# An attention and MoE kernel on one core: the 96 stores of P to scratch issued by GpSimd instead of SP, with a new table of plan shifts

## The chip, the core and the metric

The kernel runs on one core of a Trainium2 chip. Its time is the device time of one execution in microseconds. TensorE (PE) multiplies, with its weight loads shown apart (PEld); VectorE (DVE) and ScalarE (ACT) do elementwise work; SyncE (SP) issues the DMAs; GpSimd (POOL) does little. All data are float32; products are made from float32r pieces.

## The reference

Eight batches, eight heads, 512 tokens and 32 states of 64 numbers. The attention reads states by tokens and tokens by states; the results are put together and go through a bilinear feed-forward layer:

```python
def _attn_ref(x, state):                       # x: 8x8x512x64, state: 8x8x32x64
    scores = scale * np.matmul(x, state.transpose(0, 1, 3, 2))
    a = softmax(scores)
    xread = np.matmul(a, state)
    scores2 = scale * np.matmul(state, x.transpose(0, 1, 3, 2))
    a2 = softmax(scores2)
    sread = np.matmul(a2, x)
    return np.concatenate([xread, sread], axis=2)

def _moe_ref(x, w_a, w_b, w_out):              # 4352 tokens x 512, d_ff = 1536
    a = x @ w_a
    b = x @ w_b
    return a * b @ w_out
```

Here `softmax` stands for the four lines that subtract the maximum, take the exponential and divide by the sum.

## The kernel before, in words

**P.** The tokens' part of the feed-forward layer is not computed from `xread`. Since `xread = a @ state`, the kernel multiplies the states by the weights first: P = state x (w_a, w_b), for every batch and head, and then `x @ w_a` of a batch is `a @ P`. The 1536 columns of the hidden layer are cut into six chunks (c = 0 to 5) of 256 columns of w_a and w_b each. For a chunk, `chunk(c)` converts the weights (`Conv`: shifts and merges on DVE, casts on ACT, a float32 split into two float32r pieces, `wq`), then `products(c, bg)` makes P for four batches at a time (bg = 0, 1, a "half-chunk"): 8 products of 128x512 on PE into PSUM, copied by ACT into a staging buffer (`sw_st`, `wo10` or `wo11`, four in turn), and stored to DRAM, `scr{c}_{bg}`, in two DMAs of 256 KB for each buffer: 8 stores for a half-chunk, 96 in all. The store is where the layout changes: rows leave in the order of states and batches and come back batch by batch.

**Loads of P.** `Batch.load(c)` reads the 512 KB of one batch and chunk from `scr` into `p_raw`; `split` makes the pieces `p_h` (cast on ACT) and `p_l` (difference on DVE). There are 46 such loads; two of the 48 (batch, chunk) pairs are made directly (`direct0`, `direct1`).

**The two layers.** `layer1` multiplies the attention weights `at_h`, `at_l` of a batch by P's pieces into PSUM `ab`, and ACT and DVE form the product of the two halves and split it (`a_sb`, `g_h`, `g_l`). `layer2` multiplies that by the pieces of w_out (`wo0` to `wo11`) into `acc`. The table `VISITS` says which batch takes which chunks when. Partial sums of a batch go to DRAM (`part`) and come back (`stg`). A last unit does the same for the states' own rows.

**The order.** Nothing is issued as the code is written. Every call is recorded as a unit with its engine; `Recorder.cost` gives it an occupancy and a latency; `plan` works out a latest time for each unit backwards from PE's paced matmuls, adds the unit's entry of the table `SHIFTS` (in 100 ns, by the unit's number), and then puts each engine's units in an order by these times. The engines run these orders; each instruction waits by semaphores for what it reads, and each engine's queue is in order. SP's queue issues all 279 rows of DMAs, loads and stores mixed; a store that waits for its copy holds up the loads behind it. GpSimd makes an identity matrix at the start and then nothing. Nearly every instruction is issued from one line of the source, so the profile shows one line number, and the tiles' names tell the work apart.

Of the kernel before, what the change touches and what calls it, by code (L numbers as in the profile page):

```python
# [167 lines left out]
class Recorder:  # L168
# [31 lines left out]
    def cost(self, u, eng, method, out, ins, kw):  # L200
        n = 1
        sh = (out if isinstance(out, View) else ins[0]).where()[0]
        for x in sh[1:]:
            n *= x
        ps = bool(ins) and ins[0].tile.pool.name.startswith("ps")
        if eng == "PE":
            if method == "transpose" or kw.get("is_transpose"):
                o = n * .85
            elif ins[-1].dtype == F32R:
                o = (n + 32) / 2.4  # L210
            else:
                o = n / .6
            if sh[0] < P:
                o *= sh[0] / P
            if method == "matmul" and "is_transpose" not in kw and ins[-1].dtype == F32 and not u.turned:
                o, u.turned = o + 370, True
            lat = o + 172
        elif eng == "ACT":
            if method == "activation":
                o, lat = (870, 960) if "accum_out" in kw else (560, 660)  # L220
            elif ps:
                o, lat = 466 * n / 512 + (60 if n < 300 else 0), 587 * n / 512 + (80 if n < 300 else 0)
            else:
                o, lat = 522 * n / 512, 100 + n * 1.015
            if n < 8:
                o, lat = 60, 80
        elif eng == "DVE":
            if method.startswith("tensor_scalar") and not ps:
                o, lat = (65, 140) if n <= 1 else (75, 166) if n <= 16 else (333 * n / 512, 419 * n / 512)
            elif method == "tensor_reduce":  # L230
                o, lat = 593, 676
            elif method == "transpose":
                o, lat = 628, 704
            elif method == "reciprocal":
                o, lat = (72, 154) if n == 1 else (162, 244)
            else:
                o, lat = 65 + n * 1.045, 155 + n * 1.045
        elif eng == "SP":
            o = 440
            v = out if isinstance(out, View) else ins[0]  # L240
            u.bytes = 4
            for x in v.where()[0]:
                u.bytes *= x
            u.load = isinstance(out, View) and out.tile.pool.name != "dram"
            u.serve, u.land = u.bytes / 428 + (0 if u.load or u.bytes < 4e5 else 240), 1560 if u.load else 900
            lat = 980 + u.serve + u.land
        else:
            o, lat = 1000, 1060
        if eng in ("ACT", "DVE") and out.tile.name.startswith("sd_") and len(out.where()[0]) == 4:
            o, lat = 2 * o, 2 * lat  # L250
        if eng in ("ACT", "DVE"):
            o, lat = o * SLACK, lat * SLACK
        if u.calls[:-1]:
            u.lat = u.occ + lat
            u.occ += o
        else:
            u.occ, u.lat = o, lat
# [8 lines left out]
class Engine:  # L266
# [13 lines left out]


SHIFTS = {
# [12 lines left out]
}  # L295


# [164 lines left out]
def attn_moe(ctx, tc, xt, xn, sd, wl, w_out, out):  # L462
# [97 lines left out]
    nxt = []  # L560
# [40 lines left out]
    def columns(c, hp, hh):  # L601

        if c:
            return [(slice(0, 512), w[c, hp][:, hh])]
        x = hp % 2 * 256
        return [(slice(f * 256, f * 256 + 256), w[0, f, hp // 2][:, hh, x:x + 256]) for f in range(2)]
# [4 lines left out]
    def project(c, hp, bg, hh, psp, tag):  # L611
        if hh == 0:
            name, bufs = SW[st["n"] % len(SW)]
            st[bg], st["n"] = proj.tile([P, 2, 512], F32, name=name, bufs=bufs), st["n"] + 1
        sw = st[bg]
        ps = psp.tile([P, 512], F32, name=tag)
        with rec.together(sw):
            for cols, r in columns(c, hp, hh):
                for k, s in enumerate((sd_h, sd_l)):
                    nc.tensor.matmul(ps[:, cols], lhsT=s[hp // 2][:, 2 * (hp % 2) + hh, bg], rhs=r,  # L620
                                     start=(k == 0), stop=(k == 1))
        nc.scalar.copy(out=sw[:, hh], in_=ps)
        if hh:
            h = 2 * (hp % 2)
            nxt.extend(lambda i=i: nc.sync.dma_start(
                out=scr[c][bg][hp // 2, :, h + i].rearrange("b n x -> n b x"), in_=sw[:, i]) for i in range(2))


# [412 lines left out]
    def products(c, bg, where=ms):  # L1041
        for hp in range(4):
            for hh in range(2):
                project(c, hp, bg, hh, *where)
        flush()
# [126 lines left out]
```

## Time and profile before

| | us |
|---|---|
| median of three runs | 700.57 |
| the runs | 702.35, 700.57, 700.18 |
| the profiled execution | 700.03 |
| its span | 698.2 |
| PE busy | 677.7 (97%) |
| DVE busy | 486.5 (70%) |
| ACT busy | 394.3 (56%) |
| POOL busy | 0.7 |

The busy times are unions of the engines' instructions in one profiled execution; PE's ends are modelled, so that a busy PE is not necessarily at its peak. The span goes from the program's first instruction to its last. The granted TensorE clock was full (0.999). DMAs moved 134 MB, 55% of the 16 engines' time, all of the kernel's own from SP's queue. The lines of the page and of the timelines are shown with the steps that use them.

### The profile page before, as it was taken

The numbers are of one execution on the slowest core, as the hardware profiler recorded it, in microseconds if no ns is written. First come the engines' busy times: TensorE is split into PE (matmuls) and PEld (weight loads), VectorE is DVE, ScalarE is ACT, GpSimd is POOL, SyncE is SP. The second block draws the span as 40 slices with busy tenths as digits, with TensorE's granted clock in tenths as the row PEclk, the third lists the DMA queues.
The fourth block names the chain that finished last, engine by engine and source line by source line (L and its number), as shares of the span: only waits on it lengthen the run. The fifth ranks groups of instructions, "written<-read, shape, count | busy, mean of one in ns | idle before, by whom it ended". The sixth has DMA issues, their size and how long they took to land.

```text
span 698.2 us, 10183 instructions
## 1 busy us (share of the span) xinstructions
PE 677.7 (97%) x3712; PEld 543.2 (78%) x3712; DVE 486.5 (70%) x947; ACT 394.3 (56%) x727; POOL 0.7 (0%) x6
## 2 busy tenths in 40 slices
PE   4899999999999999999999999999999999999997
PEld 1576767887878888788888877877798888988886
DVE  5999788889986775745997367558869734884321
ACT  6988967898764667754543344334555433552322
POOL 0000000000000000000000000000000000000000
PEclk9999999999999999999999999999999999999999
DMA  8689977899495757768995144234244312500002
GB/s 325 243 295 336 338 248 243 307 319 393 163 335 204 271 171 251 252 232 263 392 332 158 59 155 125 95 120 139 82 152 150 109 43 61 181 31 30 1 0 92
DMA packets 55090, 134.36 MB, mean 192 GB/s; under 512 B 5632, under 2 KB 5632, under 8 KB 55040
## 3 DMA queue, kind: packets, MB, share of 16 engines
q1 hardware_dynamic: 55040, 133.71, 55.1%
q8 instruction: 29, 0.48, 0.3%
q14 instruction: 21, 0.17, 0.1%
HBM read 87.03 MB, written 46.66 MB: 191 GB/s over the span
## 4 chain that ended last, share of the span: by engine, by line
PE 88%; ACT 5%; DMA 5%; issue 1%; SPq 1%; DVE 0%; DVEq 0%
PE ab L1129 41%; PE acc L1129 38%; PE ms L1129 9%; ACT wq L1129 2%; DMA p_raw<-scr 1%; DMA p_raw<-sd 1%; DMA scr<-sw_st 1%; DMA part<-stg 1%; DMA scr<-wo 1%; SPq L1129 1%; ACT t L1129 1%; ACT sd_h L1129 0%; ACT wo L1129 0%; ACT sw_st L1129 0%; ACT g_h L1129 0%
## 5 line engine op out<-in xcount | busy, mean ns | idle before, releaser
L1129 PE MATMUL acc<-wo,g_h 128*128 128x512 f32 x816 | 249.0, 392 | 0.0
L1129 PEld LDWEIGHTS acc<-wo,g_h 128*128 128x128 f32 x816 | 151.6, 188 | 31.7 <-issue 0.8
L1129 DVE TENSOR_TENSOR a_sb<-ab,a_sb 128x512 f32<-128x512 f32 (+1 forms) x108 | 71.2, 659 | 130.2 <-PE ab L1129 115.2
L1129 PE MATMUL ab<-at_h,p_h 128*128 128x512 f32 x384 | 149.7, 394 | 2.4 <-ACT p_h L1129 2.4
L1129 PE MATMUL acc<-wo,g_l 128*128 128x512 f32 x408 | 150.9, 392 | 0.0
L1129 PE MATMUL ab<-at_l,p_h 128*128 128x512 f32 x384 | 149.6, 393 | 0.0
L1129 PE MATMUL ab<-at_h,p_l 128*128 128x512 f32 x384 | 148.8, 392 | 0.0
L1129 ACT COPY a_sb<-ab 128x512 f32<-128x512 f32 (+1 forms) x108 | 61.0, 565 | 137.6 <-PE ab L1129 137.0
L1129 ACT CAST g_h<-a_sb 128x512 fp32r<-128x512 f32 (+1 forms) x108 | 64.7, 599 | 59.5 <-DVE a_sb L1129 50.1
L1129 PEld LDWEIGHTS acc<-wo,g_l 128*128 128x128 f32 x408 | 76.6, 188 | 19.1 <-issue 2.5
L1129 DVE TENSOR_TENSOR g_l<-a_sb,g_h 128x512 fp32r<-128x512 f32 (+1 forms) x108 | 70.7, 655 | 28.1 <-ACT g_h L1129 21.3
L1129 PEld LDWEIGHTS ab<-at_h,p_h 128*128 128x128 f32 x384 | 72.2, 189 | 23.2 <-ACT p_h L1129 3.5
L1129 PEld LDWEIGHTS ab<-at_h,p_l 128*128 128x128 f32 x384 | 72.3, 189 | 16.0 <-issue 0.8
L1129 PEld LDWEIGHTS ab<-at_l,p_h 128*128 128x128 f32 x384 | 72.2, 189 | 15.3 <-issue 0.8
L1129 ACT CAST p_h<-p_raw 128x512 fp32r<-128x512 f32 x92 | 53.4, 621 | 24.5 <-PE ab L1129 16.0
L1129 DVE TENSOR_TENSOR p_l<-p_raw,p_h 128x512 fp32r<-128x512 f32 x92 | 60.1, 682 | 6.0 <-ACT p_h L1129 5.8
L1129 DVE TENSOR_SCALAR t<-t 128x512 int32<-128x512 int32 x120 | 49.6, 420 | 13.4 <-ACT t L1129 10.8
L1129 ACT CAST wq<-t 64x512 fp32r<-64x512 f32 (+1 forms) x64 | 38.7, 619 | 4.4 <-PE ab L1129 1.7
L1129 DVE SCALAR_TENSOR_TENSOR t<-raw,t 128x512 int32<-128x512 int32 (+1 forms) x60 | 39.5, 684 | 0.2
L1129 PE MATMUL ms<-wq,sd_h 128*128 128x512 f32 (+2 forms) x112 | 38.0, 412 | 0.3 <-ACT a L1129 0.2
L1129 PE MATMUL ms<-wq,sd_l 128*128 128x512 f32 (+2 forms) x112 | 37.4, 403 | 0.0
L1129 DVE TENSOR_TENSOR stg<-acc,stg 128x512 f32<-128x512 f32 x44 | 28.4, 683 | 9.2 <-PE acc L1129 9.2
(97 smaller groups left out, 671.4 us busy)
## 6 DMA issues: line engine op xcount, KB each, us to landing
p_raw<-scr SPq DMA_DIRECT2D x46, 512.0 KB, 4.0
scr<-sw_st SPq DMA_DIRECT2D x48, 256.0 KB, 5.1
scr<-wo SPq DMA_DIRECT2D x48, 256.0 KB, 4.2
raw<-wl SPq DMA_DIRECT2D x22, 512.0 KB, 6.1
part<-stg SPq DMA_DIRECT2D x20, 512.0 KB, 5.6
stg<-part SPq DMA_DIRECT2D x20, 512.0 KB, 5.0
out<-stg SPq DMA_DIRECT2D x34, 256.0 KB, 2.1
x_raw<-xt SPq DMA_DIRECT2D x14, 576.0 KB, 4.0
```

What stands on the lines that cost most here:

```text
L1129: getattr(obj, method)(*map(real, args), **{k: real(x) for k, x in kw.items()})
```

## The change

The stores of P are issued on GpSimd's queue; the recorder's cost function gets a branch for them; and the table of shifts is another one throughout, since the units are numbered anew when the stores are no longer SP's. The kernel's work is otherwise the same: the same matmuls, conversions, loads and stores.

```diff
@@ Recorder.cost
             else:
                 o, lat = 65 + n * 1.045, 155 + n * 1.045
+        elif method == "dma_start" and eng == "POOL":
+            o, lat = 1000, 3600
         elif eng == "SP":
             o = 440
...
@@ the table (16 lines before, 16 after; first line of each)
 SHIFTS = {
-    2: -1852, 7: 155, 8: 101, 12: 125, 13: -1927, 18: -166, 24: 194, 25: 125, 27: 16, 28: -291, 35: 29, 36: 59,
...
+    1: -726, 7: 339, 8: -507, 9: 151, 12: 165, 14: 29, 15: 900, 17: -215, 18: 169, 19: -256, 20: 2, 21: -113,
...
@@ project
         if hh:
             h = 2 * (hp % 2)
-            nxt.extend(lambda i=i: nc.sync.dma_start(
+            nxt.extend(lambda i=i: nc.gpsimd.dma_start(
                 out=scr[c][bg][hp // 2, :, h + i].rearrange("b n x -> n b x"), in_=sw[:, i]) for i in range(2))
```

The order moves on every engine. Three places, each as it stands in the built program (engine's rows in order; the number behind a name is the buffer's; x2 is two equal ones).

First, SP's queue around the first eight stores of P and the first loads of it, before:

```order
L1129 DMA raw_416<-wl 128x2x512
L1129 DMA scr0_0_466<-sw_st_447 32x4x512 x2
L1129 DMA scr0_0_466<-wo10_463 32x4x512 x2
L1129 DMA scr0_0_466<-sw_st_514 32x4x512 x2
L1129 DMA x_nat_557<-xn 128x1024
L1129 DMA scr0_0_466<-wo11_543 32x4x512 x2
L1129 DMA raw_594<-wl 128x2x512
L1129 DMA p_raw_627<-scr0_0_466 128x2x512
L1129 DMA p_raw_631<-scr0_0_466 128x2x512
```

SP's queue at the same place in the changed kernel:

```order
L1130 DMA raw_416<-wl 128x2x512
L1130 DMA wo6_433<-xn 128x1024
L1130 DMA raw_506<-wl 128x2x512
L1130 DMA x_nat_593<-xn 128x1024
L1130 DMA p_raw_622<-scr0_0_441 128x2x512
L1130 DMA p_raw_630<-scr0_0_441 128x2x512
```

and GpSimd's queue, which holds these stores first of all its DMAs:

```order
L1130 DMA scr0_0_441<-sw_st_427 32x4x512 x2
L1130 DMA scr0_0_441<-wo10_471 32x4x512 x2
L1130 DMA scr0_0_441<-sw_st_511 32x4x512
L1130 DMA scr0_0_441<-wo11_527 32x4x512
L1130 DMA scr0_0_441<-sw_st_511 32x4x512
L1130 DMA scr0_0_441<-wo11_527 32x4x512
```

The eight stores have left SP's queue; the same two loads, of weights and of x_nat, still stand ahead of the first loads of P.

Second, ACT's rows from the last copy of those eight products (`wo11<-acc`) to the first split of a loaded P, before:

```order
L1129 COPY wo11_543<-acc_547 128x512
L1129 ACTIVATE e2_499,m2_522<-e2_499,m2_522 128x512
L1129 COPY a_sb_580<-ab_361 128x512
L1129 ACTIVATE s_p_568<-s_p_568 128x512
L1129 ACTIVATE t1_600<-wo9_363 128x512
L1129 CAST at_h_609<-ms_584 128x512
L1129 CAST g_h_612<-a_sb_580 128x512
L1129 COPY a2_619<-ms_604 128x512
L1129 CAST at_l_623<-ms_584 128x512
L1129 ACTIVATE a2_619<-ms_633,m2_522 128x128
L1129 CAST p_h_680<-p_raw_627 128x512
```

and the last rows ahead of that split in the changed kernel:

```order
L1130 COPY stg_609<-acc_534 128x512
L1130 ACTIVATE s_p_598<-s_p_598 128x512
L1130 COPY stg_627<-acc_548 128x512
L1130 COPY sw_st_634<-ms_611 128x512
L1130 COPY stg_609<-acc_544 128x512
L1130 COPY stg_627<-acc_602 128x512
L1130 COPY sw_st_634<-ms_638 128x512
L1130 CAST at_h_659<-ms_646 128x512
L1130 CAST p_h_668<-p_raw_622 128x512
```

Four copies of sums to `stg` and two of the next half-chunk's products to `sw_st` stand ahead of the split, where before they stood behind it.

Third, DVE's rows at the last piece of chunk 0's weights (`wq_301`, now `wq_315`); `xst` is the states' result, `raw` is a load of w_out. Before:

```order
L1129 TENSOR_TENSOR sd_l1_241<-p_raw_108,sd_h1_179 128x4x4x32
L1129 TENSOR_SCALAR t1_229<-t1_229 128x512
L1129 TENSOR_SCALAR t2_325<-t1_313 128x512
L1129 SCALAR_TENSOR_TENSOR t1_229<-wo9_112,t1_229 128x512
L1129 SCALAR_TENSOR_TENSOR t2_325<-raw_196,t2_325 128x512
L1129 COPY xst_340<-ms_198 64x2x32 x2
L1129 TENSOR_SCALAR wo9_112<-t2_282 128x512
L1129 TENSOR_SCALAR t1_313<-t1_313 128x512
L1129 SCALAR_TENSOR_TENSOR wq_301<-t1_229,wo9_112 128x512
```

and in the changed kernel:

```order
L1130 TENSOR_TENSOR sd_l1_289<-p_raw_108,sd_h1_176 128x4x4x32
L1130 TENSOR_SCALAR wo9_119<-t2_284 128x512
L1130 TENSOR_SCALAR t2_343<-t1_301 128x512
L1130 SCALAR_TENSOR_TENSOR wq_315<-t1_262,wo9_119 128x512
L1130 TENSOR_SCALAR t1_301<-t1_301 128x512
L1130 TENSOR_TENSOR a_sb_341<-ab_269,a_sb_341 128x512
L1130 SCALAR_TENSOR_TENSOR t1_301<-raw_208,t1_301 128x512
L1130 SCALAR_TENSOR_TENSOR t2_343<-raw_208,t2_343 128x512
L1130 COPY xst_371<-ms_179 64x2x32
```

The two copies to `xst` and the merge and one shift of `w_out` (`t2<-raw`, `t1<-t1`) moved behind the weights' last piece.

21 rows, old and new, of the table SHIFTS are left out of this document.

## The prediction

> **What bounds the kernel now.** I read the page's first part, then the busy times in stretches that I chose by the loads of P, then the chain of waits, then the timelines of the engines that stand in it.
>
> ```profile
> span 698.2 us, 10183 instructions
> PE 677.7 (97%) x3712; PEld 543.2 (78%) x3712; DVE 486.5 (70%) x947; ACT 394.3 (56%) x727; POOL 0.7 (0%) x6
> ```
>
> PE is the bound over the whole, and GpSimd does nothing after the start. Windows (columns: length, then busy us and count of PE, weight loads, DVE, ACT, POOL, granted clock, DMA share, GB/s):
>
> ```profile
> 0.00:36.00 36.00, 22.69 (x168) 12.51 (x172) 27.07 (x59) 27.71 (x50) 0.70 (x6) 1.00 0.78 282
> 36.00:52.00 16.00, 16.00 (x164) 11.70 (x160) 15.80 (x41) 13.61 (x29) 0.00 (x0) 1.00 0.86 307
> 52.00:100.00 48.00, 45.23 (x291) 32.03 (x294) 40.65 (x85) 39.74 (x74) 0.00 (x0) 1.00 0.87 312
> 100.00:300.00 200.00, 199.56 (x986) 160.95 (x987) 158.18 (x303) 144.49 (x264) 0.00 (x0) 1.00 0.75 264
> 300.00:690.00 390.00, 390.00 (x2097) 322.80 (x2096) 242.68 (x458) 168.39 (x311) 0.00 (x0) 1.00 0.39 131
> ```
>
> From 100 us on PE idles 0.44 us in 590. So nothing can be won there, and only there where PE starves could much be lost. What can be won lies before 100 us: 13.3 us of idle PE up to 36 us, which is the start (the first loads, then DVE and ACT, each busy 27 us of it), and 2.8 us between 52 and 100. The 96 stores run from 38.5 to 328 us, so all but the first touch a stage where PE has no gap. The first gap is theirs. The chain there:
>
> ```profile
> 40.85 2.06 PE acc L1129 x16
> 42.91 3.48 DMA scr<-sw_st
> 46.59 4.67 DMA scr<-wo
> 51.28 3.67 DMA p_raw<-scr
> ```
>
> The last of the eight stores of P's first half-chunk is issued at 46.59 and lands at 51.26; the load of it follows at once and lands at 54.95. ACT and PE wait for it (in brackets: idle before, and who ended it):
>
> ```profile
> 44.68 0.59 ACT L1129 COPY wo<-acc 128x512 f32<-128x512 f32 x1 [0.21 <-PE acc L1129]
> 54.97 0.62 ACT L1129 CAST p_h<-p_raw 128x512 fp32r<-128x512 f32 x1 [3.90 <-DMA p_raw<-scr]
> 55.64 0.50 PE L1129 MATMUL ab<-at_h,p_h 128*128 128x512 f32 x1 [1.11 <-ACT p_h L1129]
> 58.84 0.66 PE L1129 MATMUL ms<-ident,e 128*128 128x128 f32 x4 [0.37 <-ACT at_l L1129]
> 87.93 0.50 PE L1129 MATMUL ab<-at_h,p_h 128*128 128x512 f32 x1 [0.92 <-ACT p_h L1129]
> 89.82 0.50 PE L1129 MATMUL ms<-wq,sd_h 128*128 128x512 f32 x1 [0.24 <-ACT a L1129]
> 285.33 0.50 PE L1129 MATMUL ab<-at_h,p_h 128*128 128x512 f32 x1 [0.36 <-ACT p_h L1129]
> ```
>
> ACT loses 3.90 us, PE 1.11 and 0.37 at once; the waits at 87.93 and 89.82 are for an ACT that is behind; that at 285.33 is a load of P again.
>
> **The change part by part.** Prices of the moved stores on SP (issue in ns, then landing in us), and of loads of P:
>
> ```profile
> L1129 SPq DMA_DIRECT2D scr<-sw_st x48: 517/524/1922, 38.5 to 328.0; - x48
> L1129 SPq DMA_DIRECT2D scr<-wo x48: 517/518/892, 39.8 to 321.2; - x48
> DMA to landing us min/median/max: 2.3/4.3/9.8
> ```
>
> GpSimd's price is in no row. Its issue p lies between SP's 0.52 and 1.92; its landing between 2.3 and 9.8. I take p = 1.0, twice SP's usual, nearer to the low end because 95 of 96 of SP's lie there. A store that is not behind SP's loads should land about midway between SP's best and its median, 3.3, and the longer issue adds 0.5: 3.8 us from the start of the issue. [...]
>
> (a) The start. DVE has four rows fewer ahead of the last piece of chunk 0's weights: a pair of copies to xst, one shift and one merge that belong to `w_out`. Their rows:
>
> ```profile
> 29.47 0.43 DVE L1129 TENSOR_SCALAR t<-t 128x512 int32<-128x512 int32 x1 [0.81 <-ACT wq L1129]
> 30.41 0.68 DVE L1129 SCALAR_TENSOR_TENSOR t<-raw,t 128x512 int32<-128x512 int32 x1
> 31.02 0.45 DVE L1129 COPY xst<-ms 64x64 f32<-64x64 f32 x2
> ```
>
> By their starts that is 0.34 + 0.60 + 0.48, so 1.4 us. ACT has 65 rows ahead of the last copy of the first eight products in both orders, so it gains what it waits less for PE:
>
> ```profile
> 26.23 0.59 ACT L1129 CAST at_h<-ms 128x512 fp32r<-128x512 f32 x1 [0.24 <-PE ms L1129]
> 31.37 0.59 ACT L1129 COPY a_sb<-ab 128x512 f32<-128x512 f32 x1 [0.80 <-PE ab L1129]
> 44.10 0.37 ACT L1129 ACTIVATE a<-ms,m 128x128 f32<-128x128 f32 x1 [0.37 <-PE ms L1129]
> ```
>
> With the 0.21 at 44.68 that is 1.6 us. I take the copies to end 1.0 us earlier, at 44.3 for 45.27; ends 0 and -1.6.
>
> (b) The first stores. The first pair and the last, which SP issues behind a load of x_nat:
>
> ```profile
> 38.55 1.20 SPq L1129 DMA_DIRECT2D scr<-sw_st  x2
> ...
> 45.33 0.55 SPq L1129 DMA_DIRECT2D x_nat<-xn  x1
> 45.98 1.16 SPq L1129 DMA_DIRECT2D scr<-wo  x2
> ```
>
> So SP needs 51.26 - 45.27 = 6.0 us from the last copy to the landing. On GpSimd the last store stands behind one other: 1.0 + 3.8 = 4.8 us, 1.2 less. With the ends of the price it is 2.8 to 11.7 us, -3.2 to +5.7. The load of 3.67 us is unchanged; SP's two loads ahead of it stay there.
>
> (c) Where PE stands at that wait. In the changed order 16 matmuls of 32x64, 5 of 128x128 and 4 of 32x512 no longer come before the first use of the loaded P, and 8 of 128x256 now do: 1.1 us less done at the same moment, +1.1. So a, b and c give -1.0 - 1.2 + 1.1 = -1.1.
>
> (d) ACT fills its wait: four copies to stg and two to sw_st stand ahead of the first split of P, where they stood behind it.
>
> ```profile
> 58.67 0.60 ACT L1129 COPY sw_st<-ms 128x512 f32<-128x512 f32 x1
> 59.68 1.08 ACT L1129 COPY stg<-acc 128x512 f32<-128x512 f32 x2
> ```
>
> Six at 0.54 are 3.2 us of the 3.90 idle. ACT comes out of this stage that much less behind, so PE's 0.37, 0.92 and 0.24 should go: -1.5; ends 0 and -1.5. What is late next is the DMA.
>
> (e) The half-chunks that are stored and loaded again in one go. PE's rows between the last product and the first use of the loaded P, counted in both orders, at 2.72/12 us for a matmul of 128x512:
>
> ```profile
> 350.45 2.72 PE ab L1129 x12
> 98.57 0.39 PE L1129 MATMUL ms<-wq,sd_l 128*128 128x512 f32 x1
> 99.61 0.52 SPq L1129 DMA_DIRECT2D scr<-wo  x1
> 102.27 0.90 SPq L1129 DMA_DIRECT2D p_raw<-scr  x2
> 109.91 0.50 PE L1129 MATMUL ab<-at_h,p_h 128*128 128x512 f32 x1
> ```
>
> For chunk 1 there were 34 such matmuls with two groups of scores, now 38 with none: about 1 us less cover. Before, the 11.1 us from 98.8 to 109.91 were enough without a wait; now there are 10.1. The store was issued at 99.61 and the load behind it could go at 102.27, 2.7 us; 3.8 is 1.1 more. In the changed order the load has one load of x_raw (576 KB) less ahead of it, 1.9 us at the 312 GB/s of that stretch. So at most 11.1 + 1.1 - 1.9 = 10.3 us are needed: +0.2 if all else is equal; I take +0.5, ends 0 and +3. Chunk 2 falls from 64 such matmuls to 49 (11.1 us), for the same need and a little more for other loads: +0.3, ends 0 and +2.5. Chunk 4 rises from 44 to 55, which takes the 0.36 at 285.33 away: -0.4. Chunks 3 (43 to 49, and scores) and 5 (60 to 54) keep 12 us or more: 0, hidden by those matmuls; without that cover each would cost what GpSimd is late.
>
> (f) SP issues 96 DMAs fewer, 50 us at 0.52. SP's time is on no path but the one in (b): 0. What it is freed for, earlier loads, still waits for buffers. GpSimd's queue holds nothing else, so a store that waits for its copy holds up later stores alone.
>
> (g) The rest of the new order, in the stage from 100 us: 0; ends -0.5 and +1, by the 0.44 us of idle there.
>
> Sum: -1.1 - 1.5 + 0.5 + 0.3 - 0.4 = -2.2 us. Against the profiled execution's 700.03 us (span 698.2 and 1.8 around it) that is 697.8. The median of the runs is 700.57, 0.5 above the profiled one; that half a us is within the runs' scatter, and I leave it out. About 0.3%, 2.1 us, is what a measurement of this kernel can tell from no change.
>
> **The rivals.** *The stores land no sooner.* The DMA engines are 0.86 busy in 36 to 52 us and 0.87 up to 100, and a store from another queue moves over the same 16. Then b is 0, and e costs 1.0 at both chunks: -1.0 + 1.1 - 1.5 + 2.0 - 0.4 = +0.2, so 700.2 us: no change. For it speaks that busy share; against it that half of SP's stores land within 4.3 us and SP's own loads stand ahead of many others.
>
> *GpSimd's issue is too slow, and the kernel slower.* The eight stores of the first half-chunk become ready from 37.5 us on (SP's first issue at 38.55, less a). From p = 1.1 on GpSimd works them off back to back and the last lands at 37.5 + 8p + 2.8; against 51.26 that is 8p - 11.0. The last pairs of chunks 1 and 2 are late by 2(p - 1) each. The sum is then 12p - 15, zero at 1.25, over +2.1 from p = 1.43, and at SP's worst, 1.92, +8.0 (708). At p = 1.6 it is 704.2. What could make p so long is DVE:
>
> ```profile
> L1129 DVE TENSOR_SCALAR t<-t 128x512 int32<-128x512 int32 x16 | 6.6, 422 | 8.8 <-ACT t L1129 7.9 <-ACT wq L1129 0.8
> ```
>
> [...] Against it: in 8 to 60 us there are only 16 of them, and from 52 us on DVE is busy 40.65 us of 48. Should GpSimd in turn hold DVE up, the same stage pays.
>
> **How the numbers follow.** My forecast, the store chain shorter and ACT less behind: 0.46, 697.8 us. The stores no sooner: 0.28, 700.2. GpSimd too slow: 0.26, around 704. Low end: a, b and d at their good ends without PE running out, about -5: 695.0. High end p = 1.6, 704.5; beyond it I leave about 1 in 10. The forecast's own range is 695.0 to 698.4. Faster 0.46, same 0.28, slower 0.26.
>
> **What would show it.** In the changed profile: the last of the first eight stores landing before 50.5 us; ACT's wait before its first split of P under 2 us; no wait of PE for ACT near 88; PE's idle from 52 to 100 us under 2 us for 2.8; store issues on POOL near 1 us, and landings near 3.8. I am wrong if POOL is busy 1.4 us or more with a store, if DVE's mean for the 512-wide TENSOR_SCALAR rises over 422 ns, or if PE waits over 1 us for p_h of chunk 1 or 2.

## The result and the profile after

| | before | after |
|---|---|---|
| median, us | 700.38 | 723.09 |
| runs, us | 699.49 to 702.35 (4) | 720.87 to 723.95 (4) |
| profiled execution, us | 700.03 | 723.95 |

The ratio is 1.0307 (95% interval 1.0276 to 1.0338): the changed kernel is 3.1% slower, 22.7 us between the medians. The prediction was 697.8, range 695.0 to 704.5. The page of the changed kernel, its first two lines and GpSimd's queue (packets, MB, share of the 16 DMA engines):

```profile
span 722.2 us, 10235 instructions
PE 689.4 (95%) x3712; PEld 544.7 (75%) x3712; DVE 486.7 (67%) x947; ACT 396.5 (55%) x727; POOL 54.9 (8%) x102
...
q0 software_dynamic: 7680, 25.17, 8.9%
```

The work is the same: 3712 matmuls, 947 and 727 rows, DVE and ACT busy as long as before. The span is 24 us longer, so PE waits or runs slowly. The same windows as in the prediction (busy us and count of PE, weight loads, DVE, ACT, POOL; then granted clock, DMA share, GB/s):

```profile
0.00:36.00 36.00, 23.84 (x147) 11.81 (x151) 26.93 (x59) 28.00 (x49) 0.70 (x6) 1.00 0.82 292
36.00:52.00 16.00, 16.00 (x157) 12.96 (x157) 15.79 (x40) 13.94 (x32) 5.26 (x9) 1.00 0.83 283
52.00:100.00 48.00, 43.20 (x281) 29.56 (x280) 37.78 (x81) 35.59 (x68) 4.95 (x9) 0.96 0.80 279
100.00:300.00 200.00, 189.32 (x933) 147.21 (x932) 147.51 (x285) 134.06 (x244) 34.68 (x62) 0.98 0.69 246
300.00:690.00 390.00, 388.88 (x2040) 318.29 (x2039) 250.87 (x473) 177.40 (x323) 9.34 (x16) 1.00 0.42 141
```

The stage from 100 to 300 us, in which PE idled 0.44 us before, now has 10.7 us of idle and a clock of 0.98; DVE and ACT do 10 us less each in it. Busy time does not carry the whole loss, so I use PE's lag: the moment at which a matmul starts, less the nominal time of all matmuls ahead of it (0.227 us for 128x512, 0.120 for 128x256, 0.109 for 128x128, and less for the narrow ones). How the lag grows, in us, in the profiled execution of five kernels (e1, e2, e9 and e12 are explained below):

| stretch | before | after | e1 | e2 | e9 | e12 |
|---|---|---|---|---|---|---|
| up to 50 us | 23.7 | 23.3 | 23.5 | 22.9 | 23.4 | 23.3 |
| 50 to 60 | 2.6 | 6.4 | 3.2 | 6.0 | 3.7 | 5.1 |
| 60 to 110 | 3.2 | 3.0 | 3.2 | 3.4 | 2.7 | 2.6 |
| 110 to 120 | 0.1 | 4.2 | 0.2 | 3.4 | 3.6 | 2.7 |
| 120 to 170 | 0.1 | 2.4 | 1.6 | 1.5 | 2.7 | 2.7 |
| 170 to 220 | 0.2 | 7.0 | 1.6 | 6.7 | 6.1 | 5.9 |
| 220 to 270 | -0.1 | 6.0 | -0.1 | 5.6 | 4.6 | 6.9 |
| 270 to the last matmul | 2.8 | 4.3 | 6.1 | 2.3 | 4.0 | 4.1 |

Of the changed kernel's 24 us, 3.8 arise where the first P is loaded, and some 19 between 110 and 270 us.

**The price of GpSimd.** The scratch tile's view: the two kinds of store with min, median and max of the issue in ns, then the landing of all the tile's transfers in us, the 96 stores and the 46 loads of P together:

```profile
L1130 POOL DMA_DIRECT2D scr<-sw_st x48: 550/552/940, 37.9 to 352.9; - x48
L1130 POOL DMA_DIRECT2D scr<-wo x48: 550/552/742, 40.9 to 340.3; - x48
DMA to landing us min/median/max: 2.3/4.5/9.6
```

DVE's 512-wide TENSOR_SCALAR in the groups by line and form (busy us, mean ns, then the idle time ahead of them and who ended it):

```profile
L1130 DVE TENSOR_SCALAR t<-t 128x512 int32<-128x512 int32 x120 | 50.3, 424 | 24.6 <-ACT t L1130 20.9 <-ACT wq L1130 2.9
```

A store costs GpSimd 0.55 us, as good as SP's 0.52. The landing row was 2.3/4.3/9.8 before, but it mixes stores and loads: its 9.8 was a load. Taken from the two traces, the 96 stores alone land after 2.3/4.9/9.6 us for SP's 2.3/4.4/8.3. DVE's mean is 424 ns, 420 before over the same 120. So GpSimd's issue is not slow, its stores land half a us later in the median, and these rows of DVE are 1% slower.

**The first P.** The last of the eight stores, SP's queue around it, and who waited (in brackets: idle before, and who ended it):

```profile
45.18 0.55 POOL L1130 DMA_DIRECT2D scr<-wo  x1
41.44 0.38 SPq L1130 DMA_DIRECT2D raw<-wl  x1
46.97 0.33 SPq L1130 DMA_DIRECT2D x_nat<-xn  x1
52.63 0.89 SPq L1130 DMA_DIRECT2D p_raw<-scr  x2
56.80 0.62 ACT L1130 CAST p_h<-p_raw 128x512 fp32r<-128x512 f32 x1 [3.81 <-DMA p_raw<-scr]
57.47 1.22 PE L1130 MATMUL ab<-at_h,p_h 128*128 128x512 f32 x2 [3.41 <-ACT p_h L1130]
```

The last store lands at 52.48, 7.30 us after its issue; the load of P follows at 52.63. The 512 KB load of weights at 41.44 went out ahead of five of the eight stores; before, SP issued the same load behind all eight, at 47.23. PE waits 3.41 us, for 1.11. That this load delays the stores is likely by the order of events, but no run moved it alone.

**The stalls behind 110 us**: in all of them PE waits for a copy or a cast of ACT. ACT and PE at 171 to 181 us:

```profile
171.88 0.59 ACT L1130 COPY sw_st<-ms 128x512 f32<-128x512 f32 x1 [5.27 <-PE ms L1130]
172.49 0.62 ACT L1130 CAST wq<-t 64x512 fp32r<-64x512 f32 x1
...
176.05 1.15 ACT L1130 CAST p_h<-p_raw 128x512 fp32r<-128x512 f32 x2
177.22 0.62 ACT L1130 CAST wq<-wq 64x512 fp32r<-64x512 f32 x1
177.87 1.14 ACT L1130 CAST wq<-t 64x512 fp32r<-64x512 f32 x2
179.03 0.66 ACT L1130 ACTIVATE t<-raw 128x512 f32<-128x512 f32 x1
179.59 0.57 ACT L1130 COPY a_sb<-ab 128x512 f32<-128x512 f32 x1
177.59 0.39 PE L1130 MATMUL ab<-at_h,p_l 128*128 128x512 f32 x1
180.21 0.77 PE L1130 MATMUL ab<-at_h,p_h 128*128 128x512 f32 x1 [2.23 <-ACT a_sb L1130]
```

ACT first stands idle for 5.27 us, because the head of its queue waits for a product of PE's that comes after a run of `layer2`. Then it works without a gap, and the copy that frees `ab` for PE stands behind four rows of conversions. PE waits 2.23 us. The same at 120.85 (2.19 us, for `a_sb` behind two casts), only that there ACT itself had waited 1.00 us for a load of P just before, at 117.76.

**The clock.** After the longest stalls the granted clock (the column ahead of the DMA share) is half for a while:

```profile
54.00:57.00 3.00, 0.06 (x1) 0.00 (x0) 0.00 (x0) 0.20 (x1) 0.00 (x0) 1.00 0.77 269
58.00:60.00 2.00, 2.00 (x8) 1.37 (x7) 1.10 (x3) 1.82 (x4) 0.00 (x0) 0.50 1.02 410
120.00:122.00 2.00, 1.15 (x5) 0.96 (x6) 0.69 (x1) 1.93 (x4) 0.00 (x0) 1.00 1.05 415
122.00:124.00 2.00, 2.00 (x7) 1.56 (x6) 1.79 (x4) 1.95 (x5) 0.00 (x0) 0.56 1.04 423
180.00:183.00 3.00, 2.79 (x7) 2.21 (x8) 2.97 (x8) 2.23 (x5) 1.09 (x2) 0.54 0.20 81
```

In the trace's record of the clock these are three stretches of 3.41 us at 0.50, at 57.4, 122.2 and 180.3; before there is none while PE works. In the timeline the matmuls at 180.78 to 182.91 start 0.43 us apart instead of 0.23. Each stretch loses up to half its length, 1.7 us: at most 5.1 of the 24 us.

### The profile page after: what moved, and what is told of

The parts are those of the page before. It is cut to its first block, busy times and chain, and to the rows that moved or that the text cites. A ratio compares the mean times of both kernels' runs of the same rounds, so it can differ in the third digit from the quotient of the medians.

```text
span 722.2 us, 10235 instructions
## 1 busy us (share of the span) xinstructions
PE 689.4 (95%) x3712; PEld 544.7 (75%) x3712; DVE 486.7 (67%) x947; ACT 396.5 (55%) x727; POOL 54.9 (8%) x102
## 4 chain that ended last, share of the span: by engine, by line
PE 49%; issue 35%; POOL 6%; ACT 4%; DMA 3%; DVE 1%; SPq 0%; POOLq 0%; DVEq 0%; ACTq 0%
PE ab L1130 25%; PE acc L1130 23%; POOL scr L1130 6%; PE ms L1130 2%; DMA raw<-wl 1%; DMA p_raw<-sd 1%; ACT wq L1130 1%; DMA p_raw<-scr 1%; ACT sd_h L1130 1%; ACT t L1130 0%; DMA scr<-wo 0%; ACT e L1130 0%; ACT a L1130 0%; ACT wo L1130 0%; DVE t L1130 0%
## 5 line engine op out<-in xcount | busy, mean ns | idle before, releaser
L1130 PE MATMUL ab<-at_h,p_h 128*128 128x512 f32 x384 | 152.0, 401 | 10.7 <-ACT a_sb L1130 5.8
L1130 PE MATMUL ab<-at_l,p_h 128*128 128x512 f32 x384 | 151.2, 397 | 0.1
L1130 DVE TENSOR_TENSOR g_l<-a_sb,g_h 128x512 fp32r<-128x512 f32 (+1 forms) x108 | 70.9, 657 | 38.1 <-ACT g_h L1130 23.4
L1130 PEld LDWEIGHTS acc<-wo,g_l 128*128 128x128 f32 x408 | 76.4, 188 | 19.6 <-issue 4.2
L1130 POOL DMA_DIRECT2D scr<-sw_st x48 | 27.7, 578 | 234.5 <-ACT sw_st L1130 197.9
```

The lines of the kernel that those rows point to most:

```text
L1130: getattr(obj, method)(*map(real, args), **{k: real(x) for k, x in kw.items()})
```

## The experiments

Theory A: the new order makes the loss. Theory B: GpSimd's queue makes it. Theory C: DVE and GpSimd disturb each other. "Before" stood at 699.7 to 700.8 in every comparison.

**e1, the queue alone.** The order of before, recorded as SP's, issued from GpSimd:

```diff
-        sync, gpsimd = Engine(rec, "SP", base.sync), Engine(rec, "POOL", base.gpsimd)
+        sync, gpsimd = Engine(rec, "SP", base.sync), Engine(rec, "SP", base.gpsimd)
...
-            nxt.extend(lambda i=i: nc.sync.dma_start(
+            nxt.extend(lambda i=i: nc.gpsimd.dma_start(
```

> The order of the kernel before on PE, DVE, ACT and SP, row for row, but the 96 stores are issued from GpSimd's queue. Theory A (the new order costs the time; GpSimd's issue of 0.55 us against SP's 0.52 and the same landing are worth next to nothing): 698.5 to 701.5 us, the copies' buffers and the loads of P as before. Theory B (GpSimd's queue costs it: its stores share rings and DMA engines with loads that SP no longer holds back, and land late): 712 us or more, with PE waits for p_h of several us behind each chunk. Theory C (DVE and GpSimd disturb each other): over 705 us, with DVE's mean times up by some per cent.

Measured: 705.45 us, ratio 1.0062 (1.0039 to 1.0085), 4.7 us slower. Between A's and B's numbers, and nearer A's; it is in C's, but the sign that C named is missing: the 120 rows of DVE shown above take 422 ns, 420 before. The first chain (start, length):

```profile
45.35 5.10 DMA scr<-wo
50.59 5.03 DMA p_raw<-scr
```

The landing of P's loads over the whole, in the view of their tile:

```profile
DMA to landing us min/median/max: 3.2/4.5/11.9
```

Two later waits, in ACT's timeline:

```profile
201.88 1.14 ACT L1129 CAST p_h<-p_raw 128x512 fp32r<-128x512 f32 x2 [2.37 <-DMA p_raw<-scr]
347.46 1.14 ACT L1129 CAST p_h<-p_raw 128x512 fp32r<-128x512 f32 x2 [2.87 <-DMA p_raw<-scr]
```

The stores land at 50.45, 0.8 us sooner than before. But the load of P takes 5.03 us for 3.67, and P is there 0.7 us later. The view holds 48 loads, two of them not of P; for the 46 of P the median is 4.4 us (4.0 before), the worst 11.9 (9.8). ACT's waits for loaded P are 16.2 us in all, 8.4 before. PE's longest wait behind 60 us, 1.82 us at 332, is not for P: a store issued at 324.29 took 7.30 us to land and held its staging buffer, which a piece of `w_out` takes next. So with nothing moved but the queue, loads of P and some stores land later; which of the transfers beside them delays them was not tried.

**e2, the order alone.** The changed kernel with its stores issued by SP, where the plan's times put them:

```diff
-        sync, gpsimd = Engine(rec, "SP", base.sync), Engine(rec, "POOL", base.gpsimd)
+        sync, gpsimd = Engine(rec, "SP", base.sync), Engine(rec, "POOL", base.sync)
```

> The order of the changed kernel on every engine, but the 96 stores are issued from SP's queue, at the places among SP's loads where the plan's times put them. Theory A (order): 720 to 732 us; no better than the changed kernel's 723, and worse where a store that waits for its copy holds up loads. Theory B (queue): about 700 to 705 us. Theory C: about 700 to 705 us.

Measured: 718.78 us, ratio 1.0248 (1.021 to 1.0287), 18.0 us slower without GpSimd. The lag grows at the same places as in the changed kernel. Its window, and the last of the first eight stores in its chain (start, length):

```profile
100.00:300.00 200.00, 190.28 (x944) 147.91 (x943) 149.12 (x287) 136.19 (x249) 0.00 (x0) 0.99 0.71 249
```

```profile
44.71 6.63 DMA scr<-wo
```

The two parts, 4.7 and 18.0, add up to the whole, 22.7. B and C fall as explanations of the bulk; A holds for the bulk, though its number for e2 was a little high: I had expected SP's queue to be no better for this order, and it is 4.3 us better, with intervals that just touch.

**e3 and e4, no table.** `SHIFTS = {}` in the changed kernel and in the kernel before.

> The changed kernel with an empty table of shifts: the plan's own order, with the stores on GpSimd at 1.0 and 3.6 us. Theory A1 (the new table's entries do the harm): below 723 us, about 710 to 718. Theory A2 (the plan's costs for the stores do it, and the table only trims): 723 to 735 us. Theory B: 723 us or above whatever the table is.

> The kernel before with an empty table of shifts. Theory A1: if the old table is worth its time on the chip and the new one is not, this stands 10 to 25 us above 700, near the changed kernel without its table; the difference of 23 us is then an old table lost. Theory A2 (the cost of the stores in the plan): this stays within 8 us of 700, well below the changed kernel without its table. Theory B says nothing of it.

Measured: e3 732.9 us, ratio 1.0448 (1.0407 to 1.0489); e4 723.98 us, 1.0318 (1.0274 to 1.0362). The old table is worth 23.6 us on its plan, the new one 9.8 on its own; the plan without a table is 8.9 worse. The window of e4, in which GpSimd does nothing and PE idles 9.0 us all the same:

```profile
100.00:300.00 200.00, 190.97 (x977) 150.00 (x976) 149.98 (x289) 132.49 (x242) 0.00 (x0) 0.97 0.73 249
```

So A1's first form, that the new table does harm, is wrong (without it the kernel is slower), and its second is right: a better table was lost. A2 holds for e3 and not for e4. (B's number for e3 is met too; e2 has shown that the queue is not the bulk.)

**e5, the stores counted in the plan's DMA model,** with the empty table:

```diff
         elif method == "dma_start" and eng == "POOL":
-            o, lat = 1000, 3600
+            o, u.load = 550, False
...
+            u.serve, u.land = u.bytes / 428, 900
+            lat = 980 + u.serve + u.land
@@ plan
-        if e == "SP":
+        if hasattr(u, "serve"):
             dma = max(dma, t + 980) + u.serve + (290 if u.load != turned else 0)
```

> The plan with an empty table, stores on GpSimd, but priced as SP's were (issue 0.55, 900 ns to land after their bytes) and counted in the plan's one DMA server with the loads. Compare with e3 (empty table, stores at 1.0 and 3.6 us outside that server: 732.9) and e4 (empty table, stores on SP: 724.0). Theory M (the plan does not see the stores' bytes, places the loads of P too late and too close to other loads, and this makes the 9 us between e4 and e3): 722 to 727 us. Theory N (the 9 us are what GpSimd's queue costs with any order, plus chance in the plan): 729 to 735 us.

Measured: 726.85 us, ratio 1.0378 (1.0355 to 1.0401). Theory M's number holds: of the 8.9 us between e4 and e3, 6.0 come from the way the plan prices the stores. Issue, landing and server were changed together, so which of them it is stays open. That e5 stands above e4 is not sure, since their intervals overlap.

**e6, e8: the old table on the new plans,** numbered as before (`n += u.eng in ("SP", "POOL") or u.eng != last`); e6 on e5's costs, e8 on the changed kernel's.

> As e5, with the table of the kernel before at the same units (numbered as there). Theory F (a table fits only the plan it was made for): 718 to 728 us, about e5's time. Theory G (the table's entries put right errors of the plan that stay the same when the stores move): 700 to 708 us, e5's time less the 23.3 us that the old table is worth on its own plan.

> The changed kernel's costs (1.0 and 3.6 us, outside the DMA server) with the table of the kernel before at the same units. Theory F: 725 to 740 us, about e3's 732.9 give or take. Theory G: about 710 us (e3 less 23.3).

Measured: e6 711.34 us, 1.0147 (1.0122 to 1.0172); e8 719.32 us, 1.0285 (1.024 to 1.0331). Neither theory's numbers were met. The old table keeps 15.5 us of its worth on the one plan and 13.6 on the other: more than the 9.8 that the new table, numbered for its plan, is worth. In e8 the lag grows by 3.3 us between 110 and 270 us, in e3 by 23.4: there the old table gives back nearly the whole stage, and most of what e8 loses, 15.1 us, arises behind 270 us.

**e7, a cost moved by 3%** (`o, lat = 1000, 3700`).

> The changed kernel with its new table and one cost moved by 3%: the stores' latency in the plan 3.7 us in place of 3.6. Theory F (the table fits only its plan): the order shifts in several places and the time moves by 3 us or more from the changed kernel's 723, likelier up. Theory G: 722 to 724 us.

Measured: 723.94 us, 1.0336 (1.0307 to 1.0364): no change from the changed kernel, theory G's number. The table was not lost by this small move.

**e9 and e10, loads of P that wait for no store,** on the changed kernel and on before. In `Batch.load` the source is replaced when the DMA is issued:

```diff
+    class Elsewhere:
+        def dma_start(out, in_):
+            return base.sync.dma_start(out=out, in_=xn[0].rearrange("g p (k a) c -> k p g (a c)", k=2)[0])
...
-            u = nc.sync.dma_start(out=raw, in_=scr...
+            u = nc.p_loads.dma_start(out=raw, in_=scr...
```

> The changed kernel, its order unchanged on every engine, but the 46 loads of P read 512 KB of xn in rows of the same 2 KB instead of scratch, so that they wait for no store (the values of P are other ones). Theory P (the way through the scratch, from copy to store to load, makes the loss): 698 to 708 us. Theory Q (the order of the rest, conversions, copies and casts in ACT's and DVE's queues, makes it): 716 to 723 us. Both in part: between, with the difference to 723 as the share of P.

> The same edit on the kernel before: what its own waits for P are worth. Its PE idle time between 52 and 100 us is 2.8 us and its waits for loaded P behind that under 1 us: both theories expect 696 to 700 us. Over 700 would mean that the edit itself costs time (loads that go out sooner and crowd the others), and e9 is then read against this run.

Measured: e9 718.4 us, 1.0258 (1.0235 to 1.028); e10 699.46 us, 0.9985 (0.9974 to 0.9995). So the way through the scratch costs the changed kernel 4.7 us and before 0.8. Most of the loss stays when P waits for no store: theory Q, in the main. The loads themselves stay: in e9 ACT waits 10.2 us for them in all, 11.9 in the changed kernel. In e9 PE waits 1.12 us for the first P instead of 3.41, and the stage behind is as slow as ever; PE's timeline and the window:

```profile
55.35 0.72 PE L1136 MATMUL ab<-at_h,p_h 128*128 128x512 f32 x2 [1.12 <-ACT p_h L1136]
```

```profile
100.00:300.00 200.00, 190.28 (x943) 148.24 (x942) 147.16 (x283) 135.62 (x247) 34.64 (x63) 0.99 0.70 249
```

**e11, the first eight stores alone** from GpSimd, in the order of before:

```diff
+        first = Engine(rec, "SP", base.gpsimd)
...
-            nxt.extend(lambda i=i: nc.sync.dma_start(
+            nxt.extend(lambda i=i: (nc.first if (c, bg) == (0, 0) else nc.sync).dma_start(
```

> The kernel before with only the eight stores of the first half-chunk on GpSimd, the order of everything else untouched. The prediction's step (b) (landing 1.2 us sooner, all of it on the path): 699.2 us. What the first half-chunk showed with all stores on GpSimd (stores landed 0.8 us sooner, but the load behind them took 5.03 us instead of 3.67): 700.4 to 701.2 us. Theory B (GpSimd's queue costs by itself wherever it runs beside SP's loads) expects about 0.4 us over before.

Measured: 701.67 us, ratio 1.0014 (0.9998 to 1.003): the same. In its profile the last store lands at 50.73 and P at 54.59, 0.4 us sooner than before, which does not show in the time; step (b) had 1.2. Up to that load its two queues hold what e1's hold, but the load took 3.71 us here and 5.03 in e1: the 0.7 us that P was late in e1 is not secured by one execution. (Its profiled execution has 6.8 us at half clock around 20 us, which before's has not; up to 50 us its lag is no longer than before's.)

**e12, fourteen rows of ACT's queue moved back** (13 by the expectation's count) behind the PSUM copy that PE waits for, in seven places; PE's, SP's and GpSimd's orders stay, and on DVE only the order of a few rows that read the moved ones changes:

```diff
+BEHIND = [([709, 959], 548), ([970, 965], 662), ([1268], 1026), ([1274, 1285, 1287], 1082),
+          ([1805, 1816], 1391), ([1808], 1335), ([1814, 1827, 1819], 1341)]
```

> The changed kernel with PE's, SP's and GpSimd's orders untouched and 13 of ACT's 726 rows moved back by a few rows, in seven places between 113 and 254 us: casts of weights (wq<-t, wq<-wq), first steps of conversions (t<-raw, t<-wo) and one stg copy go behind the PSUM copy (sw_st, a_sb or wo) for which PE stands idle. Theory Q (ACT's queue holds ready copies behind work that could wait): the seven places give 0.6 to 1.5 us each as far as the copy's source was ready, 6 to 8 us in all, and two of the three stretches of 3.4 us at half the granted clock that follow PE's stalls may go, 1.7 us each: 712 to 717 us. Theory R (ACT has that much work there in any order, and what is moved back comes due a few rows later): 720 to 724 us.

Measured: 720.82 us, 1.029 (1.0231 to 1.035), 2.3 us less than the changed kernel, with intervals that overlap. Theory R's range. The half-clock stretches at 122 and 180 us are gone, as theory Q thought they might be, but there is a new one of 3.4 us at 247. The place shown above, as it runs here:

```profile
174.42 0.57 ACT L1142 COPY a_sb<-ab 128x512 f32<-128x512 f32 x1
175.01 1.14 ACT L1142 CAST wq<-t 64x512 fp32r<-64x512 f32 x2
176.18 1.22 ACT L1142 ACTIVATE t<-raw 128x512 f32<-128x512 f32 x2
177.30 1.05 ACT L1142 COPY wo<-ms 128x512 f32<-128x512 f32 x2
175.04 0.50 PE L1142 MATMUL ab<-at_h,p_h 128*128 128x512 f32 x1 [0.40 <-ACT a_sb L1142]
177.92 0.50 PE L1142 MATMUL ms<-wq,sd_h 128*128 128x512 f32 x1 [1.22 <-ACT wo L1142]
```

The wait for `a_sb` falls from 2.23 to 0.40 us, and the rows moved back hold up the next copy instead: 1.22 us three microseconds later. It is not one misplaced row; ACT is behind in the whole burst.

**e13 and e14, the weight casts off ACT.** The 64x512 casts `wq<-t`, `wq<-wq` of `Conv.run` issued on DVE at their places, on both kernels. By the traces they are 72 casts and 43.8 us of ACT's busy time (64 and 39 by the expectation's count):

```diff
+    class OnVector:
+        def copy(out, in_):
+            return base.vector.tensor_copy(out=out, in_=in_)
...
-                nc.scalar.copy(
+                cast.copy(
```

> The changed kernel with the 64 casts of weights (wq<-t, wq<-wq, 64x512, 0.62 us each, 39 us of ACT) issued on DVE, at the same places of the order; nothing else moves. Theory R (between 110 and 270 us ACT's work comes in bursts that are longer than the cover PE has there, while DVE stands idle in the same bursts, 4.3 us busy of 10 at 110 and 5.2 of 10 at 170): 708 to 717 us. Theory S (the chains through DVE or the loads bind the bursts as much, and the casts only change queue): 719 to 730 us.

> The same edit on the kernel before, whose ACT has no such bursts behind it: 699 to 704 us by Theory R, since nothing there waits for the casts now and DVE has 30% of its time free; over 706 us would say that DVE has no room for them in this order, and e13 is then read against that.

Measured: e13 726.96 us, 1.0378 (1.0341 to 1.0415); e14 715.77 us, 1.0225 (1.0192 to 1.0258). The window of e13, then that of e14:

```profile
100.00:300.00 200.00, 192.48 (x957) 149.50 (x956) 172.23 (x342) 110.22 (x205) 35.08 (x62) 0.98 0.70 247
```

```profile
100.00:300.00 200.00, 195.48 (x989) 154.12 (x981) 174.54 (x345) 111.27 (x205) 0.00 (x0) 0.99 0.72 252
```

DVE, now busy 172 and 175 us of 200, has no room for the casts: in e14 PE waits 4.6 us for `a_sb` from DVE and 4.3 once for a piece of weights. Both missed theory R's numbers, and e13 is in S's. The edit costs the kernel before 15.8 us and the changed one 3.9, so the latter may get something back for it. The lag says where: in both the edit adds about 5 us up to 50 us, at the first weights; between 110 and 270 us it adds 7.8 us to the kernel before, while the changed kernel's lag falls from 19.6 to 14.6. This speaks for ACT's casts as a part of what binds the bursts, some 5 us of it. Whether the bursts are bound by ACT alone stays open.

No version that loads P beat the kernel before.

## Why the prediction was wrong, by its steps

**The step that failed is (g)**: the rest of the new order from 100 us, taken as 0 with ends -0.5 and +1. I read "PE idles 0.44 us in 590" as a property of the stage. It is a property of the old order: the old table alone is worth 23.6 us (e4), and e4's lag grows by 18 us between 110 and 270 us, 15.8 of them from 170 us on, mostly where the changed kernel's does. The waits that PE has there are others (the longest 3.40 us for `xst` and 2.36 for `wo`), so what the two share is a lost order, and not one misplaced copy. The account by edits, from medians: before 700.4; without its table 724.0; stores on GpSimd with the same prices 726.9; with the plan's flat price 732.9; with the new table 723.1.

- (a) The copies of the first products end at 44.8 instead of 45.3, -0.5 us where I had -1.0: inside its ends.
- (b) From the last copy to the landing it took 7.7 us, not 4.8. The price of the issue, the thing I worried about, was 0.55 and not 1.0. What I missed is that in the new order a load of weights goes out among the stores. In e2, with SP issuing everything in this order, the last store still takes 6.63 us (44.71 to 51.34) of the 7.30, so most of it is the order of loads and stores, not the engine. The landing that I took, 4.3 in the median and 9.8 at worst, was that of stores and loads together; SP's stores alone had 4.4 and 8.3.
- (c), (d) ACT did fill its wait with the stg copies, but the wait did not shrink (3.81 us for 3.90), since P came 1.8 us later. Between 60 and 110 us PE's lag grows by 3.0 us, 3.2 before: -0.2 for the -1.5 of (d).
- (e) Chunk 1 cost 4.1 us more between 110 and 120 us, where I had +0.5 with an end of +3; chunk 2's stretch 6.8 more, +0.3 with an end of +2.5. The count of covering matmuls was right and did not decide: with loads of P that wait for no store (e9) 3.6 and 6.1 us of lag remain. I had counted PE's cover for the transfer and not ACT's work in it.
- (f) SP's 96 issues less were not worth 0 but +4.7 us (e1): with the stores on a queue of their own the 46 loads of P landed after 4.4 us in the median for 4.0, at worst after 11.9 for 9.8.
- Clock: no step had it. It fell to 0.50 for 3.41 us after PE's wait of 3.41 us for the first P, and as much after the waits of 2.19 and 2.23 us at 120 and 180 us. The three half-clock stretches begin 19 and 17 times 3.41 us apart, and in the 3.41 us right ahead of each PE idles 98, 59 and 65%.

The rivals: *the stores land no sooner* was right on that (the stores' median 4.9 us for 4.4) and its 700.2 wrong, by (g). *GpSimd's issue is too slow* had the right sign and the wrong mechanism: its p was 0.55 against the 1.43 at which it would have decided (1.49, had its sum held the -0.8 of (c), (d) and chunk 4). No run shows the p of 1.6 that its 704.2 and the high end of my range used. DVE, to which it put a long issue down, was 67% busy, and still 87 of the 96 issues take 550 to 563 ns, the longest 940. Nor does GpSimd show in DVE's times: the 424 ns are 420 before and 423 in e2, in which GpSimd issues no store.

Of the signs named ahead, those for the forecast failed (landing 52.48 for under 50.5, ACT's wait 3.81 for under 2, PE idle 4.8 us from 52 to 100 for under 2, the issue 0.55 us for 1.0). One held: PE has no wait for ACT near 88 us. Of those against it, DVE's mean is 424 ns, over the 422 named, but DVE's busy time in all is 486.7 us for 486.5; the others did not show: POOL's issue is 0.55 us, and PE's waits of 2.2 us in the stretches of chunks 1 and 2 are for `a_sb`. It was wrong in a way that it had not named.

## What to carry to other kernels

When a change replaces a tuned order, the gaps that are not there before belong to that order, and the new one must be priced as if untuned: first ask what the old tuning is worth (here 23.6 us of 700, found by one run without it), and give the forecast that loss as its bad end. Moving DMAs to another queue also takes away the order between them and the first queue's loads; ask which loads had been held back behind them, and whom they meet now (here a 512 KB load of weights that went out at 41.44 us for 47.23, ahead of five of the eight stores). A stall of PE as long as the three here, 2.19 to 3.41 us, is to be priced with what followed each of them, 3.41 us at a clock of 0.50, up to 1.7 us by the spacing of the matmuls.

## What the runs showed of the hardware

- In the changed kernel the record of the clock has three stretches of 3.41 us at 0.50 and, between and behind them, full clock for 61.44, 54.61 and 539.3 us, 18, 16 and 158 times 3.41. In all 16 traces (before, after and the 14 runs) the changes of the clock lie whole multiples of 3.41 us apart; the stretches at half clock were 3.4, 6.8, 10.2 and, in e3, 17.1 us in one piece at 173 us. e3 has 30.7 us of it in all, e1 and e10 none while PE works. Divided into pieces of 3.41 us by these changes, from 25 us to the last matmul, the changed kernel has 98, 59 and 65% of idle PE in the three pieces that half clock followed, and at most 38% in the others; before has at most 33%, and no half clock while PE works. Counted over the 16 traces, 28 pieces at full clock had PE idle over half the time, and half clock followed all of them; it followed four others, at 43 to 49%, and none under 43%. e1's wait of 1.96 us at 56 fell into a piece with 47% of idle, and the clock stayed full (1.00 from 50 to 70 us). (PE's ends are modelled, so these shares are rough. What makes the clock fall was not tried.)
- GpSimd issues a 256 KB store in 0.55 us (550 to 1135 ns over e1 and the changed kernel), and it lands after 2.3 us at best, 4.9 in the median and 9.6 at worst, for SP's 2.3, 4.4 and 8.3.
- The same order with the stores on a second queue moved the median landing of the loads that depend on them from 4.0 to 4.4 us (e1, one profiled execution each), and the time by +0.6%.
